# A fused attention, ELU and Mish kernel: the due times of its list scheduler moved by seeded noise

## The chip, the core and the metric

The kernel runs on one core of a Trainium2 chip. The metric is device time in microseconds (us) of one launch, the median of three runs. Five engines run side by side: PE (TensorE, matrix products and transposes), DVE (VectorE), ACT (ScalarE), POOL (GpSimd) and SP (SyncE, which here issues most DMAs). Each works off its own queue in the order in which the program was written, and waits where an operand or a buffer is not ready.

## The reference

```python
def _attn_ref(x, state):                       # x 4 x 8 x 512 x 64, state 4 x 8 x 32 x 64
    scale = 1.0 / np.sqrt(D)
    a = softmax(scale * np.matmul(x, state.transpose(0, 1, 3, 2)))
    xread = np.matmul(a, state)
    a2 = softmax(scale * np.matmul(state, x.transpose(0, 1, 3, 2)))
    sread = np.matmul(a2, x)
    return np.concatenate([xread, sread], axis=2)

def _moe_ref(x, w_in, w_out):                  # 2176 x 512, 512 x 2048, 2048 x 512
    h = x @ w_in
    g = np.where(h > 0.0, h, np.exp(np.minimum(h, 0.0)) - 1.0)
    return g @ w_out

def _moe2_ref(x, w_in, w_out):
    h = x @ w_in
    sp = np.where(h > 20.0, h, np.log1p(np.exp(np.minimum(h, 20.0))))
    return (h * np.tanh(sp)) @ w_out

x = attn(x, state)       # tokens and states attend to each other
x = x.transpose(0, 2, 1, 3).reshape(B * S, H * D)
out = moe2(moe(x))       # an ELU layer, then a Mish layer
```

(softmax stands for the reference's own lines: maximum off, exponential, division by the sum.)

## The kernel before, in words

The tokens of the four batches are four blocks (b = 0 to 3) of 512, and the 4 x 32 states make one small part more. For each block the kernel reads x in two halves of the heads (`load_x`, tile xb), transposes it on PE (xT, L641), forms the scores against the states (`score_tiles`, L653), copies them out (raw, L299, a helper that copies or casts on DVE or ACT), takes the softmax over the states on DVE and ACT (prob, L665 to L678) and transposes the result (L680; tile pT for b > 0, x for b = 0). It doesn't multiply the softmax by the states: it folds the states into the first weights (`fold`, L574), which gives m, and then h = softmax x m.

The ELU layer runs in steps of 128 of the 2048 hidden units for one block: `mm1` (h0, h1, ..., L782 to L793), `hidden` (ACT's exponential and a relu, DVE's e at L814, ACT's cast and DVE's low part, g), and `mm2` (L841 to L850), which adds g times w_out into four accumulators acc0 to acc3. The products are split: a value is a high part (fp32r) and a low part, so one product is three matmuls (such as L848, L849, L850). The first steps take whole fp32 values instead (L782, L841). The states' own reading (exT, sr, own, sT, L702 to L736) comes in between. Weights arrive as 64-bit floats and are turned into fp32 by two ACT instructions (wy L461, wv L463) and DVE's L466 and L478 or L503; the tiles w1_0 to w1_3 hold w_in of the ELU layer, each the source of one fold per block.

The Mish layer runs on two halves of the tokens in eight pairs of hidden tiles, with seven products per pair (prod, L1018) in the place of eight, and adds g times w_out into accA and accB (L1057 to L1059). Copies such as u2__0_1 (L1044, in the profile under u__0_1_832) take a product out of its bank. The last pieces of g are transposed on PE (turn16_0 to turn16_3, L1219) and multiplied last.

Every instruction is written through `Plan`, a list scheduler that runs on the host while the program is built. `add` registers an operation with its engine (or both DVE and ACT, EITHER: the scheduler takes the one that comes first), an assumed cost, and the tiles that it reads and writes. `dues` goes back from the end and gives each operation a due time: the earliest of what its successors allow, or a time given by hand from the table T of the steps. `run` then lays the program out in assumed time, always the operation that can start first, and of those with one start the one with the smaller due time:

```python
                    k = (t + late, due, seq, t)
```

PSUM has eight banks: two named "att" (xT, folds and others), two "h", and one for each of acc0 to acc3; an operation that has to place a tile waits until a bank of that tag is free. The two buffers wv serve the conversion of weights, and later hold u2 and c11 of the pairs. What stands on which place of an engine's queue is fixed when the program is built; on the chip it runs in that order whatever really is late.

## Time and profile before

| | before |
|---|---|
| median of 3 runs | 721.77 us (721.12 to 722.47) |
| profiled execution | 722.41 us, span 720.5 us |
| PE busy | 701.7 us, 97% |
| DVE busy | 556.7 us, 77% |
| ACT busy | 495.8 us, 69% |
| POOL busy | 3.0 us |
| DMA | 106.83 MB |

The profile is of one execution. Its span runs from the first to the last instruction, the time around it (1.9 us) belongs to the launch. A busy time counts instructions by their modelled lengths, and matmuls overlap, so a matmul of 0.39 us can follow the one ahead after 0.23 us. A timeline gives in brackets how long the engine stood idle ahead of an instruction and what released it.

### The profile page before, as it was taken

To read this page: it belongs to the slowest core of one execution; us is meant where nothing else is said; L and a number is where in the kernel's file an instruction comes from. 1 tells how busy PE (TensorE), PEld (TensorE's weight loads), DVE (VectorE), ACT (ScalarE), POOL (GpSimd) and SP (SyncE) were. 2 spreads that over 40 slices of the span, in tenths; PEclk is the share of its full clock that TensorE was granted. 3 is DMA by queue.
4 is the path that set the end of the run, shared out by engine and by line. 5 is a ranking of instruction groups with operands and counts; after the bars stand their busy time and mean duration, and the time that the engine had idled before them with its cause. 6 is when DMAs were issued, how large, how long until landed. Compare 5 with 4: busy or idle time off the path is not lost.

```text
span 720.5 us, 10191 instructions
## 1 busy us (share of the span) xinstructions
PE 701.7 (97%) x3698; PEld 546.3 (76%) x3698; DVE 556.7 (77%) x949; ACT 495.8 (69%) x861; POOL 3.0 (0%) x14
## 2 busy tenths in 40 slices
PE   5899999999989999999999999999999999999997
PEld 3345777777757778978887888878888888888886
DVE  6899988869879985447889998769738887767622
ACT  4797999768778776467868786669347666666522
POOL 0000000000000000000000000000000000000000
PEclk9799999999999999999999999999999999999999
DMA  9965556773685647106486454642035444401001
GB/s 224 276 180 138 128 174 227 234 234 99 209 258 167 200 146 246 51 20 229 164 279 225 150 147 127 221 163 58 1 117 147 136 127 125 142 27 58 15 1 58
DMA packets 65717, 106.83 MB, mean 148 GB/s; under 512 B 6660, under 2 KB 45572, under 8 KB 65668
## 3 DMA queue, kind: packets, MB, share of 16 engines
q1 hardware_dynamic: 63444, 105.53, 47.8%
q10 hardware_dynamic: 2224, 0.66, 0.4%
q8 instruction: 29, 0.48, 0.3%
q14 instruction: 20, 0.16, 0.1%
HBM read 78.38 MB, written 27.79 MB: 147 GB/s over the span
## 4 chain that ended last, share of the span: by engine, by line
PE 90%; DVE 7%; ACT 1%; issue 0%; DVEq 0%; ACTq 0%
PE prod L1018 20%; PE acc_acc L848 7%; PE acc_acc L850 7%; PE acc_acc L849 7%; PE accB L1057 4%; PE accB L1059 4%; PE accB L1058 4%; PE accA L1057 4%; PE accA L1059 4%; PE accA L1058 4%; PE h L791 3%; PE h L793 3%; PE h L792 3%; PE fold L574 2%; PE h L772 2%; PE acc_acc L841 2%
## 5 line engine op out<-in xcount | busy, mean ns | idle before, releaser
L1018 PE MATMUL prod<-x_t,pair 128*128 128x512 f32 x384 | 96.9, 390 | 0.5 <-ACT u__0_1_832_3916 L1044 0.5
L848 PE MATMUL acc_acc<-g,w_out 128*128 128x512 f32 x232 | 93.1, 401 | 0.0
L850 PE MATMUL acc_acc<-g,w_out 128*128 128x512 f32 x232 | 90.5, 390 | 0.0
L849 PE MATMUL acc_acc<-g,w_out 128*128 128x512 f32 x232 | 90.4, 390 | 0.0
L1018 PEld LDWEIGHTS prod<-x_t,pair 128*128 128x128 f32 x384 | 71.6, 188 | 15.5 <-ACT u__0_1_832_3916 L1044 1.0
L1018 PE MATMUL prod<-x_b,pair 128*128 128x512 f32 x288 | 72.4, 389 | 0.0
L976 ACT ACTIVATE e<-u,two 128x512 f32<-128x512 f32 x68 | 48.7, 722 | 21.7 <-DVE u L975 21.6
L1018 PEld LDWEIGHTS prod<-x_b,pair 128*128 128x128 f32 x288 | 54.1, 188 | 11.2
L814 DVE SCALAR_TENSOR_TENSOR e<-e,h 128x512 f32<-128x512 f32 x62 | 42.3, 683 | 25.5 <-ACT e L807 25.0
L806 ACT ACTIVATE e<-h 128x512 f32<-128x512 f32 x68 | 40.3, 595 | 26.2 <-PE h L793 17.3
L848 PEld LDWEIGHTS acc_acc<-g,w_out 128*128 128x128 f32 x232 | 43.7, 188 | 16.2 <-issue 5.4
L817 ACT CAST g<-e 128x512 fp32r<-128x512 f32 x62 | 38.4, 621 | 25.5 <-PE acc_acc L850 19.8
L978 DVE TENSOR_TENSOR u<-u,e 128x512 f32<-128x512 f32 x68 | 46.2, 687 | 12.0 <-ACT e L977 11.8
L818 DVE TENSOR_TENSOR g<-e,g 128x512 fp32r<-128x512 f32 x62 | 42.4, 685 | 14.6 <-ACT g L817 14.0
L850 PEld LDWEIGHTS acc_acc<-g,w_out 128*128 128x128 f32 x232 | 43.5, 188 | 9.3
L807 ACT ACTIVATE e<-e,one 128x512 f32<-128x512 f32 x68 | 49.2, 725 | 1.5
L1057 PE MATMUL accB<-w_out,g 128*128 128x512 f32 x128 | 50.0, 390 | 0.0
L849 PEld LDWEIGHTS acc_acc<-g,w_out 128*128 128x128 f32 x232 | 43.6, 188 | 8.4
L1059 PE MATMUL accB<-w_out,g 128*128 128x512 f32 x128 | 49.9, 390 | 0.0
L1058 PE MATMUL accA<-w_out,g 128*128 128x512 f32 x128 | 49.8, 389 | 0.0
L1059 PE MATMUL accA<-w_out,g 128*128 128x512 f32 x128 | 49.8, 389 | 0.0
L1058 PE MATMUL accB<-w_out,g 128*128 128x512 f32 x128 | 49.8, 389 | 0.0
(300 smaller groups left out, 1472.5 us busy)
## 6 DMA issues: line engine op xcount, KB each, us to landing
pair<-wi2d SPq DMA_DIRECT2D x64, 512.0 KB, 4.0
raw_out<-in_moe_w_out SPq DMA_DIRECT2D x32, 512.0 KB, 4.4
wi2d<-comb SPq DMA_DIRECT2D x64, 256.0 KB, 2.9
raw_in<-in_moe_w_in SPq DMA_DIRECT2D x32, 256.0 KB, 5.7
raw_in<-in_moe_w_in SPq DMA_DIRECT2D x16, 512.0 KB, 4.4
xb<-in_x SPq DMA_DIRECT2D x16, 256.0 KB, 4.9
x2d<-o SPq DMA_DIRECT2D x16, 256.0 KB, 3.9
out<-o SPq DMA_DIRECT2D x13, 256.0 KB, 2.5
```

The costliest lines, as they stand in the source:

```text
L807: add("ACT", act(n) + 0.12, lambda: nc.scalar.activation(E(), E(), AF.Relu, bias=one, scale=-1.0), r=[e, "one"], w=[e])
L814: add("DVE", dve(n), lambda: nc.vector.scalar_tensor_tensor(E(), E(), -1.0, Hh(), ALU.mult, ALU.max), r=[e, h], w=[e])
L818: add("DVE", dve(n), lambda: nc.vector.tensor_tensor(g[:, 1, :n], E(), g[:, 0, :n].bitcast(F32), ALU.subtract), r=[e, (g, 0)], w=[(g, 1)])
L848: nc.tensor.matmul(acc.t, lhsT=st[:, 0, :], rhs=mv[:, 0, :], start=fst, stop=False)
L849: nc.tensor.matmul(acc.t, lhsT=st[:, 0, :], rhs=mv[:, 1, :], start=False, stop=False)
L850: nc.tensor.matmul(acc.t, lhsT=st[:, 1, :], rhs=mv[:, 0, :], start=False, stop=lst)
L976: add("ACT", act(S) + 0.12, lambda: nc.scalar.activation(e.t, u.t, AF.Ln, bias=two), r=[u, "two"], w=[e])
L978: add("DVE", 0.69, lambda: nc.vector.tensor_tensor(u.t, u.t, e.t, ALU.mult), r=[u, e], w=[u])
L1018: nc.tensor.matmul(bank.t, lhsT=w[:, pos, a, c], rhs=x[b][:, k, :], start=first and k == i == 0, stop=k == 1 and i == 2, skip_group_check= ...
L1057: nc.tensor.matmul(acc.t, lhsT=g[:, 0, cols], rhs=w[:, 0, :], start=fst, stop=False)
L1058: nc.tensor.matmul(acc.t, lhsT=g[:, 0, cols], rhs=w[:, 1, :], start=False, stop=False)
L1059: nc.tensor.matmul(acc.t, lhsT=g[:, 1, cols], rhs=w[:, 0, :], start=False, stop=lst)
```

## The change

The scheduler's rule of choice stays, but each operation's due time gets a shift. `shifts` goes through a table MOVES of 41 pairs (seed, time). A pair draws, from its seed, a span of 6, 15 or 30 us, a size of 1, 3, 8 or 20 us and a share of 2, 10 or 30%; that share of the operations whose due time lies within the span after the given time is moved by Gaussian noise of that size. The table was found by laying the program out on the host. Of the 41 times 14 lie below 60, 6 from 110 to 209, 9 from 320 to 377, 7 from 406 to 478 and 5 above 628. Second, `go` (once part of `run`) counts PE's mode changes: folds, scores and the states' products use 32-row tiles (mode=1), and the first operation of the other mode costs 0.09 (in) or 0.2 (out) more in assumed time; their own assumed costs are lowered for it. Third, `combine` names its operands' writers as predecessors. The rest makes the layout repeatable and quicker to compute. A filler of PE's gaps, which was switched off, is gone.

```diff
+INTO, OUT_OF = 0.09, 0.2
+MOVES = ((75118, 15.0), (37424, 20.5), (643, 25.2), (75746, 1.9), (30105, 6.6), (37635, 33.7), (41153, 30.7), (49481, 4.2), (3259, 37.4), (47714, 34.4), (99535, 58.8), (1855, 44.2), (56018, 54.5), (88942, 41.2), (59791, 110.1), (52383, 208.2), (23200, 178.9), (15004, 167.9), (91882, 181.8), (18113, 161.2), (20944, 353.0), (89527, 345.3), (66176, 375.8), (92493, 376.6), (76941, 320.4), (42889, 369.3), (68313, 348.7), (27382, 356.5), (3732, 353.0), (87073, 460.2), (93436, 406.0), (26739, 418.9), (55693, 443.5), (55858, 447.2), (21623, 477.8), (29573, 460.3), (85558, 628.6), (12285, 659.9), (62500, 655.4), (81304, 657.9), (63908, 660.6))
...
-    def add(self, engs, cost, fn, r=(), w=(), due=None, lag=0.0, after=(), place=()):
+    def add(self, engs, cost, fn, r=(), w=(), due=None, lag=0.0, after=(), place=(), mode=0):
...
-    def run(self, take, dma):
-
-        self.dues(dma)
+    def go(self, dma, shift, take=None, until=1e9):
...
-                ready.setdefault(e, []).append((op.due, op.seq, t, op))
+                ready.setdefault(e, []).append((due, op.seq, t, op, wait))
...
+            due = op.due + shift.get(op.seq, 0.0)
...
-            if e == "PE" and t < COLD_UNTIL:
-                c *= COLD
+            op.at = t
+            if e == "PE":
+                if t < COLD_UNTIL:
+                    c *= COLD
+                if op.mode != mode:
+                    c += INTO if op.mode else OUT_OF
+                    mode = op.mode
...
+    def shifts(self, moves):
+
+
+        shift = {}
+        for seed, a in moves:
+            rng = random.Random(seed)
+            span, sd, share = rng.choice((6, 15, 30)), rng.choice((1, 3, 8, 20)), rng.choice((0.02, 0.1, 0.3))
+            for op in self.ops:
+                if a <= op.due < a + span and rng.random() < share:
+                    shift[op.seq] = shift.get(op.seq, 0.0) + rng.gauss(0, sd)
+        return shift
+
+    def run(self, take, dma):
+        self.dues(dma)
+        self.go(dma, self.shifts(MOVES), take)
+        assert self.end < math.inf, "stuck"
...
-    add("DVE", 3.2, make_ident, w=["ident"], due=-50.0)
+    add("DVE", 2.4, make_ident, w=["ident"], due=-50.0)
...
-            add("DVE", 0.43, lambda: nc.vector.tensor_tensor(o(), a(), b(), op), r=r, w=w, place=[sa, sb])
+            add("DVE", 0.43, lambda: nc.vector.tensor_tensor(o(), a(), b(), op), r=r, w=w, place=[sa, sb],
+                after=[plan.writer[a1], plan.writer[a2]])
...
-            A("PE", 0.1 + mm(4 * step * P), lambda j=j: f(j), w=[(pt, j) for pt in pts], place=[*ms, *pts],
+            A("PE", 0.05 + mm(4 * step * P), lambda j=j: f(j), mode=1, w=[(pt, j) for pt in pts], place=[*ms, *pts],
...
-        A("PE", 0.65, score_tiles, r=[(xT, 0), (xT, 1), ("sd", b)], w=ps, lag=lag, place=held)
+        A("PE", 0.45, score_tiles, mode=1, r=[(xT, 0), (xT, 1), ("sd", b)], w=ps, lag=lag, place=held)
...
-        A("PE", 1.0, read, r=[(xb, 0), (xb, 1), exT], w=[pt])
+        A("PE", 0.5, read, mode=1, r=[(xb, 0), (xb, 1), exT], w=[pt])
```

What moves is read from the order of the instructions on each engine. A row is the line, the operation, output and inputs, and the shape; the last number of a name is a serial number, which shifts between the two programs. Lines of the changed kernel are up to 40 higher.

The first place is the start of PE's queue: the first transposes of block 0 (xT12, xT13, xT21, xT22), those of the states (st2 to st4) and the first scores. Before:

```order
L641 MATMUL xT12_127<-ident_69,xb0_5_102 128x128 x4
L641 MATMUL xT13_133<-ident_69,xb0_5_102 128x128 x4
L411 MATMUL st2_139<-ident_69,st_raw1_100 128x128 x2
L411 MATMUL st3_146<-ident_69,st_raw1_100 128x128 x2
L641 MATMUL xT21_150<-ident_69,xb0_16_107 128x128 x4
L653 MATMUL scores14_157<-xT7_128,sd0_77 32x256
...
L641 MATMUL xT22_172<-ident_69,xb0_16_107 128x128 x4
L411 MATMUL st4_184<-ident_69,st_raw1_100 128x128 x4
L653 MATMUL scores23_194<-xT17_151,sd0_77 32x256
```

With the change:

```order
L679 MATMUL xT12_124<-ident_69,xb0_5_102 128x128 x4
L448 MATMUL st2_133<-ident_69,st_raw1_100 128x128 x2
L448 MATMUL st3_137<-ident_69,st_raw1_100 128x128 x2
L679 MATMUL xT13_141<-ident_69,xb0_5_102 128x128 x4
L448 MATMUL st4_147<-ident_69,st_raw1_100 128x128 x4
L679 MATMUL xT21_155<-ident_69,xb0_16_107 128x128 x4
L691 MATMUL scores14_163<-xT7_125,sd0_77 32x256
...
L691 MATMUL scores24_200<-xT17_156,sd0_77 32x256
L679 MATMUL xT160_227<-ident_69,xb153_153 128x128 x4
L612 MATMUL fold142_248<-w1_0_28_240,sd0_77 32x128
```

Both pairs of state transposes now stand ahead of xT13, st4 ahead of xT21, and xT160, the transposes of the first half of block 1's tokens, between the scores and the first fold.

The second place is DVE's queue up to pT175, the transposed softmax of the second half of block 1's tokens. Before, its last twelve rows:

```order
L689 TENSOR_TENSOR x1_1_154_636<-pT164_640,x1_1_154_636 128x512
L818 TENSOR_TENSOR g227_659<-e226_630,g227_659 128x512
L665 STREAM_TRANSPOSE prob167_647<-raw168_648 128x512
L671 TENSOR_REDUCE mx169_649<-prob167_647 128x16
L672 TENSOR_TENSOR prob167_647<-prob167_647,mx169_649 128x512
L466 SCALAR_TENSOR_TENSOR wv100_674<-wy99_673,wv100_674 128x512
L478 SCALAR_TENSOR_TENSOR w1_2_86_661<-wy92_607,wv93_608 128x4x128
L675 TENSOR_REDUCE sm170_650<-prob167_647 128x16
L676 TENSOR_SCALAR sm170_650<-sm170_650 128x16
L677 RECIPROCAL sm170_650<-sm170_650 128x16
L678 TENSOR_TENSOR prob167_647<-prob167_647,sm170_650 128x512
L680 STREAM_TRANSPOSE pT175_732<-prob167_647 128x2x2x128
```

With the change:

```order
L703 STREAM_TRANSPOSE prob167_622<-raw168_623 128x512
L852 SCALAR_TENSOR_TENSOR e226_615<-e226_615,h7_221_600 128x512
L709 TENSOR_REDUCE mx169_624<-prob167_622 128x16
L710 TENSOR_TENSOR prob167_622<-prob167_622,mx169_624 128x512
L503 SCALAR_TENSOR_TENSOR wv85_612<-wy84_611,wv85_612 128x512
L856 TENSOR_TENSOR g219_663<-e218_602,g219_663 128x512
L713 TENSOR_REDUCE sm170_625<-prob167_622 128x16
L856 TENSOR_TENSOR g227_680<-e226_615,g227_680 128x512
L714 TENSOR_SCALAR sm170_625<-sm170_625 128x16
L715 RECIPROCAL sm170_625<-sm170_625 128x16
L716 TENSOR_TENSOR prob167_622<-prob167_622,sm170_625 128x512
L718 STREAM_TRANSPOSE pT175_698<-prob167_622 128x2x2x128
```

The weight words wv100 and the piece of w1_2 no longer stand between the softmax's rows; g219 and e226, which stood higher, do.

The third place is PE around the fold of w1_2 for block 2 (fold474, fold475), the transposes of block 3's tokens (xT503, xT504, xT514, xT515) and their scores. Before:

```order
L574 MATMUL fold474_2192<-w1_2_86_661,sd2_79 32x512
L574 MATMUL fold475_2193<-w1_2_86_661,sd2_79 32x512
L641 MATMUL xT503_2220<-ident_69,xb496_2055 128x128 x4
L641 MATMUL xT504_2229<-ident_69,xb496_2055 128x128 x4
L848 MATMUL acc1_2_acc2_534_2237<-g494_2036,w_out1_0_193_390 128x512
...
L653 MATMUL scores506_2252<-xT498_2221,sd3_80 32x256
L641 MATMUL xT514_2268<-ident_69,xb508_2069 128x128 x4
L641 MATMUL xT515_2275<-ident_69,xb508_2069 128x128 x4
L848 MATMUL acc1_2_acc3_535_2283<-g494_2036,w_out1_0_193_390 128x512
```

With the change:

```order
L612 MATMUL fold475_2111<-w1_2_86_733,sd2_79 32x512
L829 MATMUL h34_525_2129<-x1_2_293_1792,m2_0_0_384_1770 128x512
...
L831 MATMUL h40_589_2367<-x1_2_293_1792,m2_8_1_473_2113 128x512
L679 MATMUL xT515_2374<-ident_69,xb508_2125 128x128 x4
L829 MATMUL h40_589_2367<-x1_2_293_1792,m2_8_0_472_2112 128x512
...
L888 MATMUL acc1_2_acc0_532_2145<-g581_2334,w_out1_6_75_618 128x512
L679 MATMUL xT514_2395<-ident_69,xb508_2125 128x128 x4
L886 MATMUL acc1_2_acc1_533_2155<-g581_2334,w_out1_6_75_618 128x512
...
L691 MATMUL scores517_2414<-xT509_2375,sd3_80 32x256
L829 MATMUL h41_606_2429<-x1_2_293_1792,m2_8_0_472_2112 128x512
L830 MATMUL h41_606_2429<-x1_2_293_1792,m2_8_0_472_2112 128x512
L831 MATMUL h41_606_2429<-x1_2_293_1792,m2_8_1_473_2113 128x512
L679 MATMUL xT504_2436<-ident_69,xb496_2107 128x128 x4
```

The fold is now followed by step 34's h, the transposes come 110 rows later and one by one, and three matmuls of h41 stand between the scores and the next transposes.

## Rows read from the trace of the kernel before

**Rows 1.** The page: the chain that ended last, shares of the span by engine.

```profile
PE 90%; DVE 7%; ACT 1%; issue 0%; DVEq 0%; ACTq 0%
```

**Rows 2.** The table by windows: busy us (instructions) per engine, granted clock, DMA share, GB/s.

```profile
11.00:15.30 4.30, 0.82 (x12) 0.17 (x9) 4.09 (x9) 3.26 (x8) 0.00 (x0) 1.00 1.14 223
15.30:25.70 10.40, 6.77 (x38) 2.28 (x38) 8.68 (x18) 5.86 (x14) 0.00 (x0) 0.51 1.09 277
...
50.00:80.00 30.00, 28.58 (x174) 16.36 (x174) 29.14 (x54) 25.18 (x48) 1.16 (x2) 1.00 0.57 145
...
200.00:215.00 15.00, 13.03 (x99) 8.19 (x98) 10.65 (x18) 10.30 (x22) 0.21 (x1) 1.00 0.84 265
...
sum 720.50, PE 701.70 PEld 546.34 DVE 556.70 ACT 495.78 POOL 3.03; mean PE 53.98 PEld 42.03 DVE 42.82 ACT 38.14 POOL 0.23
```

**Rows 3.** Timeline of PE, 69 to 77 us: start, length, instruction, idle time before it.

```profile
69.26 0.39 PE L849 MATMUL acc_acc<-g,w_out 128*128 128x512 f32 x1
...
70.84 0.39 PE L850 MATMUL acc_acc<-g,w_out 128*128 128x512 f32 x1
71.16 1.09 PE L574 MATMUL fold<-w,sd 64*32 64x512 f32 x16
73.00 0.50 PE L791 MATMUL h<-x,m 128*128 128x512 f32 x1 [0.75 <-ACT x L299]
73.73 0.50 PE L792 MATMUL h<-x,m 128*128 128x512 f32 x1 [0.23 <-DVE x L689]
...
76.72 0.50 PE L791 MATMUL h<-x,m 128*128 128x512 f32 x1 [0.44 <-DVE e L814]
```

**Rows 4.** Timeline of PE, 201 to 209 us.

```profile
201.85 1.09 PE L574 MATMUL fold<-w,sd 64*32 64x512 f32 x16
204.40 1.25 PE L641 MATMUL xT<-ident,xb 128*128 128x128 f32 x8 [1.46 <-DVE m L588]
...
208.36 1.09 PE L641 MATMUL xT<-ident,xb 128*128 128x128 f32 x8 [0.52 <-ACT raw L299]
```

**Rows 5.** Timeline of PE at three later waits.

```profile
242.96 0.33 PE L736 MATMUL sT<-ident,own 128*128 128x128 f32 x1 [0.27 <-DVE own L730]
...
382.03 1.65 PE L1018 MATMUL prod<-x_t,pair 128*128 128x512 f32 x6 [0.55 <-ACT u__0_1_832_3916 L1044]
...
661.74 0.65 PE L1219 MATMUL turn<-ident,g 128*128 128x128 f32 x4 [0.56 <-DVE g L987]
```

**Rows 6.** Timeline of PE in the first 30 us.

```profile
7.30 1.08 PE L411 MATMUL st<-ident,st_raw 128*128 128x128 f32 x4
...
8.93 0.66 PE L653 MATMUL scores<-xT,sd 64*32 64x256 f32 x16
...
15.31 0.49 PE L574 MATMUL fold<-w,sd 64*32 64x128 f32 x2 [3.32 <-DVE w L478]
...
20.36 2.08 PE L782 MATMUL h<-x,m 128*128 128x512 f32 x2 [1.17 <-DVE x L680]
...
26.75 1.13 PE L782 MATMUL h<-x,m 128*128 128x512 f32 x2
```

**Rows 7.** Timeline of DVE in the first 24 us.

```profile
22.10 0.70 DVE L680 STREAM_TRANSPOSE x<-prob 128x512 f32<-128x512 f32 x1
```

**Rows 8.** Timeline of DVE, 71 to 76 us.

```profile
71.19 0.71 DVE L680 STREAM_TRANSPOSE pT<-prob 128x512 f32<-128x512 f32 x1
...
75.98 0.68 DVE L814 SCALAR_TENSOR_TENSOR e<-e,h 128x512 f32<-128x512 f32 x1
```

**Rows 9.** Groups of DVE instructions: busy us, mean ns, idle time before.

```profile
L478 DVE SCALAR_TENSOR_TENSOR w<-wy,wv 128x512 uint32<-128x512 uint32 x16 | 10.8, 678 | 0.2
...
L299 DVE COPY xT<-xT 128x512 f32<-128x512 f32 x3 | 2.1, 689 | 4.0 <-PE xT L641 4.0
...
L299 DVE COPY sd<-st 128x256 f32<-128x256 f32 x2 | 0.8, 419 | 0.9 <-PE st L411 0.9
```

**Rows 10.** Timeline of ACT around 381 us.

```profile
381.39 0.59 ACT L1044 COPY u__0_1_832_3916<-prod 128x512 f32<-128x512 f32 x1 [0.62 <-DVE w_out L503]
```

More of the change, by code (lines that the diff above doesn't have):

```diff
@@ L2 @@
 import math
+import random
 from contextlib import ExitStack
@@ L71 @@
 class Op:
-    __slots__ = ("engs", "cost", "fn", "preds", "succs", "bufs", "due", "n", "end", "lag", "seq")
+    __slots__ = ("engs", "cost", "fn", "preds", "succs", "bufs", "due", "n", "end", "lag", "seq", "need", "key", "mode", "at")
 class Plan:
@@ L141, in run @@
         link = 0.0
+        LAT = self.LAT
+        for op in self.ops:
+            op.n, op.end = op.need, None
+            for b in op.bufs:
+                b.t, b.left, b.end = None, b.uses, 0.0
         def open_op(op):
@@ L153, in run @@
         todo = len(self.ops)
+        mode, pe, idle = 0, [], 0.0
         while todo:
@@ L157, in run @@
                 at = free.get(e, 0.0)
-                cand, first = None, None
-                for due, seq, t, op in lst:
-                    if op.end is not None:
+                slow = e in ("DVE", "ACT")
+                if e in dma and link - BACKLOG > at:
+                    at = link - BACKLOG
+                if best and at > best[0][0]:
+                    continue
+                for due, seq, t, op, wait in lst:
+                    if t < at:
+                        t = at
+                    if best and t > best[0][0]:
@@ L178, in run @@
                     late = 0.0
-                    if e in ("DVE", "ACT"):
-                        late = LAZY if due - t > FAR else 0.0
+                    if slow:
+                        if due - t > FAR:
+                            late = LAZY
                         if e == "DVE" and len(op.engs) > 1 and at > 80.0:
@@ L232, in run @@
             for x in op.engs:
-                ready[x] = [q for q in ready[x] if q[3] is not op]
+                lst = ready[x]
+                for i, q in enumerate(lst):
+                    if q[3] is op:
+                        del lst[i]
+                        break
             for s in op.succs:
```

91 lines of the change are left out of this document (43 added, 48 removed).

## The prediction

> **What bounds the kernel now.** I read the page first, for the chain that ended last: TensorE (PE) holds 90% of it, VectorE (DVE) 7% [rows 1]. Then the table by windows, whose last line says that PE is busy 701.7 of 720.5 us [rows 2]. So PE is the bound over the run as a whole, and another order of the same work can only win back time in which PE issues nothing, at most some 19 us. The windows also say where that time lies. After the first 26 us PE falls visibly short in two stretches, 28.58 of 30 us in 50 to 80 and 13.03 of 15 us in 200 to 215. In 50 to 80 DVE is busy 29.14 of 30 us: there DVE is the bound, and PE waits for it. Last the timeline of PE at each such place, which names the wait.
>
> A 128x512 matmul issues every 0.226 us: the eight from 69.26 to 70.84 are 1.58 us for seven steps. The first one after a wait lasts 0.50 instead of 0.39 us [rows 3], so I charge each wait its idle time and 0.11 us. The profiled execution took 722.41 us, 1.9 more than its span of 720.5; the median of the three runs is 721.77, 0.64 lower. The sum is formed against 722.41, and 0.64 taken off at the end.
>
> **What the waits are worth.** After the start they are these.
> - A, 71 to 77 us: behind a fold PE waits 0.75 us for ScalarE's (ACT's) cast of the second half of block 1's tokens, 0.23 us for DVE's low part of it, and further on 0.44 us for DVE's e of step 8 [rows 3]. With 3 x 0.11 that is 1.75 us.
> - B, 201 to 208 us: a fold, right behind it two transposes xT, then scores, and two more xT. Both pairs need the two "att" banks that the work ahead of them still holds: 1.46 us until DVE has read the fold (m), and 0.52 us until ACT has copied the scores (raw) [rows 4]. With 2 x 0.11 that is 2.2 us.
> - Later: 0.27 us at 242.96 (sT needs DVE's own), 0.55 us at 382.03 (product t3 needs the bank that ACT's copy u2__0_1 empties), 0.56 us at 661.74 (the fourth turn needs DVE's g) [rows 5]. With 0.11 each: 0.38, 0.66 and 0.67 us.
>
> Together 5.7 us; this is the most that another order can return after the start.
>
> **What the change does at each place.** The work, the tiles and the number of matmuls (2647 rows of PE's order) are as before. Positions move, and some copies change between DVE and ACT.
>
> *Start: 0 us (-1 to +1).* PE waits here: 3.32 us before the fold at 15.31, then for x [rows 6]. The granted clock is 1.00 in 11.0 to 15.3, where PE is busy 0.82 of 4.3 us, and 0.51 in 15.3 to 25.7, the lower of its two levels, 1.2 GHz [rows 2]. The change puts st2 and st3 ahead of xT13. They start at 7.30 and last 1.08 us [rows 6], and they wait for the states, which arrive only then; so xT13 starts after 8.2 us, and the first scores, now at 8.93, come about 0.9 us later, by xT13's own transposes and its copy. That is the loss. On the other side DVE, which is filled from 11 us on (4.09 of 4.3, then 8.68 of 10.4 us [rows 2]), loses one weight word of 0.6 us from ahead of the second transpose x at 22.10 [rows 7] and gains a copy of about the same. So x stays near 22.1. Both ends are cushioned: from 26 us to A PE runs without a wait, and there it waits for DVE, so up to 1.7 us of delay on PE alone is taken up at A, and an earlier start of PE alone brings nothing.
>
> *A: -0.8 us (0 to -1.75).* DVE is full, so what counts is the work queued on it ahead of pT175, at 71.19 [rows 8]: 119 instructions before, 117 after. Five whole-tile words leave (wv93, wv100, two pieces of w1_2, the low part of w_out 5), 0.68 us each; of copies and casts six leave and nine come, two of the three more at 0.42 and one xT at 0.69 [rows 9]. That is -3.4 + 1.5, about -1.8 us at the pace of a full queue. It would remove the first two waits, 1.2 us. But the e of step 8, at 75.98 now [rows 8], moves up only from place 123 to 122 of the queue, so the third wait stays and may grow by 0.2; and a group of three matmuls (0.68 us) that PE ran after A now comes ahead of it, where it may wait itself. I take 0.8, less than half of the bound.
>
> *B: -2.0 us (-1.2 to -2.2).* The fold of w1_2 goes ahead by some 40 matmuls and is followed by h34, which reads an m finished long before; the transposes of block 3 come 110 rows later, with no fold near, the first between two halves of h40. The pair behind scores now has three matmuls, 0.68 us, in between, more than the 0.52 waited. So neither wait has its cause left; 0.2 stays for the two pairs' own use of the banks.
>
> *242 us: -0.2 (0 to -0.38).* sT now comes three matmuls after the last product of the states (sr) instead of six. The chain from sr to own is as long, so part of the wait may stay.
>
> *382 us: -0.6 (0 to -0.66).* ACT's copy u2__0_1 was idle 0.62 us for DVE's conversion w_out [rows 10], since both use the two buffers wv. After the change that conversion no longer stands right ahead of it. Against it: the last steps of the ELU layer now alternate with the first products of the Mish layer, which must find their banks empty.
>
> *661 us: -0.6 (0 to -0.67).* Before, the four turns stand in a row, and the fourth waits. After, turn16_0 comes six matmuls earlier, and turn16_3 stands behind nine matmuls of the last part, 2.0 us more for DVE's g.
>
> *New waits: +0.5 (0 to +2).* The tokens of block 2 are the tightest: between their scores and the second half of h32 PE has 42 matmuls, one fold and a few transposes, some 12.7 us, where it had 15.2, and DVE has to do a chain of ten instructions in it, beside the others in its queue. Two folds stand 12 matmuls (2.7 us) apart, and casts and differences of the first take some 2. The acc of step 3 may wait 0.6 us for its weights. I expect one of these to bite.
>
> *Mode changes: 0.* From the last L850 to the fold at 71.16 is 0.32 us instead of 0.226 [rows 3]: entering a stretch of 32-row matmuls costs 0.09 us. PE has 33 such stretches before and 35 after, and the two more lie ahead of 25 us, where PE waits anyway. The Trainium skill, "TensorEngine Tiling (Array Packing)", Key Properties, says that a change of the tiling mode drains the engine; the 0.09 us agrees with it. By that rule alone, two stretches more, the change would cost time: at some 0.2 us for both ends of one, +0.4 us.
>
> Sum: 0 - 0.8 - 2.0 - 0.2 - 0.6 - 0.6 + 0.5 = -3.7 us. 722.41 - 3.7 = 718.7 for a profiled execution, 718.1 us as a median.
>
> **The rivals.**
> - *All waits go.* A loses its third wait too, nothing new appears, and DVE gains up to 1 us at the start, which A passes on: 721.77 - 5.7 - 1 = 715.1. Against it: DVE's queue is as full as before, and e of step 8 hardly moves. One more way leads here: two h matmuls take 2.08 us at 20.36, at the low clock, and 1.13 at 26.75 [rows 6]. If the four transposes xT160, now put into the idle stretch between scores and fold, kept the clock up, over 0.95 us would come back on PE, though A would take most of it. The Trainium skill, "TensorE: Matmul & The Clock Gate", Part 4, says that transposes don't count as busy for the clock, which speaks against that; no trace here shows it yet.
> - *Waits only move.* The 5.7 us are waits for DVE and ACT, whose work is unchanged. Where PE arrives earlier it waits later: at h32 (up to 2), the first Mish products (up to 1), the acc of step 3 (0.6). Then the 3.7 are paid back: 721 to 722. For it: DVE's 29.14 of 30 us. Against it: in 200 to 215 DVE is busy 10.65 of 15 us [rows 2], so B was a matter of order, not of load.
> - *Slower: the start.* One mechanism: the first scores wait for the states behind st2 and st3. If the first x comes over 1.7 us later, A's cushion is used up, and each further us shows, since DVE's whole queue moves back with it; the low clock also lasts longer, 0.95 us per pair of h matmuls. Three us late with two more pairs at the low clock is 3 + 1.9 - 1.7 = 3.2, less B's 2.0: +1.2 and more, 723 to 724. It decides from some 2.5 us of delay at the scores; I count 0.9.
>
> **How the numbers follow.** A measurement of this kernel can tell about 0.2%, 1.44 us, from no change. Likeliest is the sum, with some terms off: 0.62, with a range of its own of 716.8 to 720.3. All waits go: 0.12. Waits only move: 0.16, most of it within 1.44 us. Slower: 0.10. Faster by over 0.2% takes the first two and a little of the third, 0.77; same 0.13; slower 0.10. The range reaches from the rival with all waits gone, 715.0, to near the middle of the second, 721.5.
>
> **What would show it.** Right: no PE wait behind a fold for DVE's m around 200 us, and PE near 15 of 15 us there; the waits for the fourth turn and for u2__0_1 gone; at A the cast of x no longer waited for, but e of step 8 still. Wrong: a PE wait for the tokens of block 2, or for acc near 60 us; the first fold or h over a microsecond later than 15.3 and 20.4; a low clock that lasts beyond 26 us.

## The result, and the profile after

The changed kernel takes 715.19 us (median of 4 runs, 714.15 to 716.58), the kernel before beside it 721.44 us (721.02 to 722.47): a ratio of 0.9912, 95% interval 0.9888 to 0.9937. That is 6.25 us less, where 3.7 were forecast; 715.19 lies just inside the range (715.0 to 721.5) and close to the rival that all waits go (715.1). The four runs fall into two groups, 714.15 and 714.23, 716.15 and 716.58; the experiments below show where that comes from. The profiled execution is one of the slower two, 716.58 us with a span of 714.6.

The page of the changed kernel: busy time by engine, and the chain that ended last, which answers to [rows 1].

```profile
PE 700.1 (98%) x3698; PEld 547.1 (77%) x3698; DVE 557.3 (78%) x951; ACT 493.3 (69%) x859; POOL 3.5 (0%) x14
...
PE 97%; DVE 1%; DMA 1%; ACT 0%; issue 0%
```

PE holds 97% of the chain and DVE 1%, where they held 90% and 7%. The table by windows answers to [rows 2]: busy time (instructions) of PE, PE's weight loads, DVE, ACT and POOL, then the granted clock, the DMA share and GB/s.

```profile
11.00:15.30 4.30, 3.70 (x40) 1.54 (x39) 3.12 (x6) 2.53 (x6) 0.00 (x0) 1.00 1.13 240
15.30:25.70 10.40, 4.67 (x36) 1.82 (x37) 10.40 (x22) 6.84 (x15) 0.00 (x0) 0.70 1.10 265
...
50.00:80.00 30.00, 30.00 (x173) 17.25 (x172) 29.55 (x55) 24.00 (x46) 1.16 (x2) 1.00 0.45 123
...
200.00:215.00 15.00, 15.00 (x68) 12.43 (x67) 10.28 (x17) 10.44 (x17) 0.00 (x0) 1.00 0.81 244
```

Both stretches in which PE fell short are full, 30.00 of 30 and 15.00 of 15 us. DVE is as busy in 50 to 80 us as before, 29.55 us for 29.14. PE's waits of the whole run, grouped, tell the same: every line belongs to the first 22 us.

```profile
PE fold L612 <- DVE w L515: 4.7, 1, 4.7
PE warm L410 <- DVE ident L396: 3.1, 1, 3.1
PE h L820 <- DVE sm L715: 1.4, 1, 1.4
PE st L448 <- DMA st_raw<-in_state: 0.9, 1, 0.9
PE scores L691 <- ACT xT L339: 0.3, 1, 0.3
```

The timeline of PE at A, which answers to [rows 3]:

```profile
66.32 1.09 PE L612 MATMUL fold<-w,sd 64*32 64x512 f32 x16
67.33 0.50 PE L886 MATMUL acc_acc<-g,w_out 128*128 128x512 f32 x1
...
72.24 0.39 PE L829 MATMUL h<-x,m 128*128 128x512 f32 x1
72.47 0.39 PE L830 MATMUL h<-x,m 128*128 128x512 f32 x1
...
74.97 0.60 PE L751 MATMUL exT<-ident,raw 128*128 128x128 f32 x4
75.37 0.50 PE L829 MATMUL h<-x,m 128*128 128x512 f32 x1
```

A fold stands at 66.32 and is over some five microseconds ahead of the h at 72.24; before, a fold stood right ahead of the h that waited. The h matmuls from 72.24 on follow each other at 0.23 us. The timeline of DVE there, which answers to [rows 8]:

```profile
69.24 0.71 DVE L718 STREAM_TRANSPOSE pT<-prob 128x512 f32<-128x512 f32 x1
...
74.64 0.68 DVE L852 SCALAR_TENSOR_TENSOR e<-e,h 128x512 f32<-128x512 f32 x1
```

pT came 1.95 us earlier (69.24 against 71.19) and the e of step 8 1.34 us earlier (74.64 against 75.98). The remaining places on PE, which answer to [rows 4] and [rows 5]:

```profile
188.27 1.09 PE L612 MATMUL fold<-w,sd 64*32 64x512 f32 x16
189.29 0.50 PE L829 MATMUL h<-x,m 128*128 128x512 f32 x1
...
192.23 1.09 PE L612 MATMUL fold<-w,sd 64*32 64x512 f32 x16
...
218.56 0.60 PE L679 MATMUL xT<-ident,xb 128*128 128x128 f32 x4
...
246.95 0.27 PE L774 MATMUL sT<-ident,own 128*128 128x128 f32 x1
...
657.54 0.60 PE L1257 MATMUL turn<-ident,g 128*128 128x128 f32 x4
657.89 0.48 PE L1095 MATMUL acc<-w_out,g 128*128 128x512 f32 x1
```

The folds are each followed by h matmuls, the transposes stand one by one, and sT and the turns have no wait in front.

**A ledger.** A timeline's brackets count only idle time past the modelled end of an instruction. So I also went through PE's queue and added up the step at which each kind of matmul issues when nothing holds it (0.227 us for a 128x512 of a split product, 0.43 for one of whole fp32, 0.109 for a transpose). The time on the clock minus that sum is the time lost so far. Here it is at several times, for the kernel before, and for each other run as its difference to before; the e-numbers are the experiments below. In the last two rows the added transposes (38 and 42 of 0.109 us) have been put back, so that all rows mean the same. The first column is the least certain, since the folds and the clock of the start weigh most there.

```
at us                  30     70     80    200    260    360    390    470    500    670
before, lost        19.81  25.26  27.85  31.70  36.39  37.45  38.23  38.11  38.71  40.09
changed kernel        0.1    0.8   -1.4   -1.2   -4.2   -4.2   -5.0   -5.0   -5.6   -6.3
e1 (the same)        -1.2   -1.8   -4.0   -3.9   -6.8   -6.8   -7.6   -7.6   -8.2   -8.9
e2                   -0.7   -0.9   -3.1   -2.9   -5.9   -5.9   -6.7   -6.7   -7.3   -8.0
e8                   -0.6   -0.2   -2.4   -2.1   -5.0   -5.0   -5.8   -5.8   -6.5   -7.1
e6 (120 to 285)       0.2    0.5    0.5    0.7   -2.1   -2.1   -2.1   -2.1   -2.1   -2.1
e7 (from 285)        -0.5   -1.0   -1.0   -1.0   -1.0   -1.0   -1.8   -1.8   -2.4   -3.1
e12 (up to 285)      -1.0   -1.3   -3.5   -3.3   -6.3   -6.3   -6.3   -6.3   -6.3   -6.3
e10                  -0.3    0.1   -2.1   -1.9   -4.9   -4.9   -5.7   -5.7   -6.3   -7.0
e11                  -1.1   -1.7   -1.5   -1.4   -1.4   -1.4   -1.4   -1.4   -1.4   -1.4
```

The changed kernel gains 2.2 us at A (between 70 and 80), 3.0 between 200 and 260, 0.8 at 382, 0.6 between 470 and 500, and 0.7 at 661. In between, the difference moves by 0.2 us at most. The order of before isn't one row of zeros either: e6 and e7 have it up to 120 and 285 us, and stand 0.5 behind and 1.0 ahead of the trace of before at 70 us. The end (from the last matmul to the end of the span) went from 4.1 to 4.4 us.

### The profile page after: what moved, and what is told of

Same layout as the page of the kernel before. It is cut to its first block, busy times and chain, and to the rows that moved or that the text cites. A ratio compares the mean times of both kernels' runs of the same rounds, so it can differ in the third digit from the quotient of the medians.

```text
span 714.6 us, 10194 instructions
## 1 busy us (share of the span) xinstructions
PE 700.1 (98%) x3698; PEld 547.1 (77%) x3698; DVE 557.3 (78%) x951; ACT 493.3 (69%) x859; POOL 3.5 (0%) x14
## 4 chain that ended last, share of the span: by engine, by line
PE 97%; DVE 1%; DMA 1%; ACT 0%; issue 0%
PE prod L1056 21%; PE acc_acc L886 8%; PE acc_acc L888 7%; PE acc_acc L887 7%; PE accA L1095 4%; PE accB L1096 4%; PE accA L1096 4%; PE accB L1097 4%; PE accB L1095 4%; PE accA L1097 4%; PE h L829 4%; PE h L831 4%; PE h L830 4%; PE acc_acc L879 3%; PE h L820 2%; PE fold L612 2%
## 5 line engine op out<-in xcount | busy, mean ns | idle before, releaser
L1016 DVE TENSOR_TENSOR u<-u,e 128x512 f32<-128x512 f32 x68 | 46.5, 688 | 16.0 <-ACT e L1015 15.3
```

What stands on the lines that cost most here:

```text
L1016: add("DVE", 0.69, lambda: nc.vector.tensor_tensor(u.t, u.t, e.t, ALU.mult), r=[u, e], w=[u])
```

## The experiments

Throughout, theory 1 is that each place is worth the wait that goes there and the parts add up; theory 2 is that waits only move, because DVE's and ACT's work is the same. For the start, theory 1 is that its length passes to the end of the run, theory 2 is the prediction's cushion at A.

**e1, the same kernel again.** No edit.

> The changed kernel once more, for its size and its spread: its four runs lay at 716.2 to 716.6 twice and at 714.2 twice. Theory 1 (the two levels come from the start, where the granted clock rises once early, once late; in the profile at hand it rises at 12.65 us, before it rose at 8.61): a profile at 714.2 shows the first scores and the first h up to 2 us earlier and everything after 30 us as in the profile at hand. Theory 2 (a wait in the middle that appears in some executions): the start is the same in both, and one wait of some 2 us after 30 us is there in the slower one only.

714.15 us (714.09 to 716.16), 0.9896 (0.9879 to 0.9912), again in two groups, three executions near 714.1 and one at 716.16. The median lies below the range of the prediction. The profiled execution is now one of the faster, with a span of 712.1. Two timelines of PE's start, first the changed kernel's, then e1's:

```profile
7.29 1.09 PE L448 MATMUL st<-ident,st_raw 128*128 128x128 f32 x4 [0.93 <-DMA st_raw<-in_state]
...
10.87 1.11 PE L691 MATMUL scores<-xT,sd 64*32 64x256 f32 x16
...
19.66 0.68 PE L612 MATMUL fold<-w,sd 64*32 64x128 f32 x16 [4.69 <-DVE w L515]
21.70 2.04 PE L820 MATMUL h<-x,m 128*128 128x512 f32 x2 [1.37 <-DVE sm L715]
```

```profile
7.28 0.63 PE L448 MATMUL st<-ident,st_raw 128*128 128x128 f32 x4 [0.98 <-DMA st_raw<-in_state]
...
9.17 0.66 PE L691 MATMUL scores<-xT,sd 64*32 64x256 f32 x16
...
17.52 0.68 PE L612 MATMUL fold<-w,sd 64*32 64x128 f32 x16 [2.41 <-DVE w L515]
19.56 2.05 PE L820 MATMUL h<-x,m 128*128 128x512 f32 x2 [1.36 <-DVE sm L715]
```

The instructions are the same. In the first the four transposes st take 1.09 us, in e1 0.63, and the first scores 1.11 and 0.66. I read this as the two levels of the clock: the first still ran at the lower one past 10 us, e1 had left it by 7.28. (The granted clock reads 1.00 in both there; only the durations tell them apart.) The scores come 1.7 us earlier in e1, and the first h 2.1. From the first scores to the first h it is 10.8 and 10.4 us, and before it was 11.4 (8.93 to 20.36 [rows 6]): DVE is busy in most of it, 9.54 of the 10.83 us in the first and 9.61 of 10.39 in e1, and its instructions from 12.07 us on (9.93 in e1) stand 2.1 us earlier throughout. So an early rise at 7 us reaches the first h by way of DVE, and the ledger shows 2.6 us between the two executions at 70 us and the same 2.6 at 670.

**e2, xT13 ahead of the state transposes again.**

```diff
+        xt13, sts = self.first
+        for st in sts:
+            st.preds.append(xt13)
+            st.need += 1
+            xt13.succs.append(st)
...
```

> The changed kernel with the first transposes of PE in the order of before (xT13 ahead of the states' st2 and st3, st4 behind xT22); nothing else on PE, DVE or ACT moves beyond these. Theory 1 (the states' transposes ahead of xT13 delay the first scores from 8.93 to 10.87 us and the first h from 20.36 to 21.70, and nothing takes that up, since the changed order has no wait left at 72 us): 1 to 2 us faster than the changed kernel, about 713 to 714. Theory 2 (the delay is taken up by DVE's full queue up to 80 us, as the prediction held for the kernel before): no difference, 714 to 716.5.

714.78 us (714.41 to 715.85), 0.9900 (0.9886 to 0.9914): no difference. Its first scores at 8.65 and first h at 19.36 are earlier than e1's, but its low clock ended at 25.2 us where e1's ended at 23.2.

**e3, only the moves from 110 to 209.**

```diff
-MOVES = ((75118, 15.0), (37424, 20.5), (643, 25.2), (75746, 1.9), (30105, 6.6), (37635, 33.7), (41153, 30.7), (49481, 4.2), (3259, 37.4), (47714, 34.4), (99535, 58.8), (1855, 44.2), (56018, 54.5), (88942, 41.2), (59791, 110.1), (52383, 208.2), (23200, 178.9), (15004, 167.9), (91882, 181.8), (18113, 161.2), (20944, 353.0), (89527, 345.3), (66176, 375.8), (92493, 376.6), (76941, 320.4), (42889, 369.3), (68313, 348.7), (27382, 356.5), (3732, 353.0), (87073, 460.2), (93436, 406.0), (26739, 418.9), (55693, 443.5), (55858, 447.2), (21623, 477.8), (29573, 460.3), (85558, 628.6), (12285, 659.9), (62500, 655.4), (81304, 657.9), (63908, 660.6))
+MOVES = ((59791, 110.1), (52383, 208.2), (23200, 178.9), (15004, 167.9), (91882, 181.8), (18113, 161.2))
```

> The changed planner with only the six moves at times 110 to 209 kept. B is then as in the changed kernel (the fold of w1_2 ahead, the transposes of block 3 far behind it), and the Mish layer's end as before. By the ledger of the two traces (waits at 201 to 243 us are worth 2.9 us): 718.5 if the start and 71 to 77 us stay as before; the waits at 382, 484 and 661 us stay in the profile, about 0.8, 0.6 and 0.7 us. If the wins hang together (a later stretch moved by all that comes ahead), under 717 or over 720.

724.54 us (722.59 to 727.49), 1.0037 (1.0025 to 1.0049): slower, on the side on which the wins were to hang together (over 720). PE's waits at 200 to 215 us are gone. Two others are there that neither kernel has, and the wait for the e of step 8 is longer than before (1.1 for 0.44 us), in the grouped waits of PE:

```profile
PE prod L1056 <- ACT u__0_2_856_4064 L1082: 2.3, 1, 2.3
PE prod L1056 <- ACT u__0_4_900_4356 L1082: 1.1, 1, 1.1
PE h L829 <- DVE e L852: 1.1, 1, 1.1
```

By the same sums, which the table leaves out, e3 gains 2.7 us between 200 and 260 us and keeps them to 360, close to the 2.9 expected; it loses 0.8 ahead of 70 us, 0.3 at A and 4.1 between 390 and 470. So the waits at B were not paid back; the new ones come from places where a shorter table leaves another order. The table isn't a sum of edits: a subset of it lays the whole program out anew. No run has the changed scheduler with an empty table, so how much of the order is owed to the noise and how much to the new assumed costs stays open. To test parts, the finished orders had to be cut and joined instead (e5 on).

**e4, only B's edit.** Kernel before, with block 3's transposes held back behind steps 38 and 39.

```diff
+STEPS = ((38, 1), (39, 1))
...
+        for hf, op in self.later:
+            p = self.steps[STEPS[hf]]
+            op.preds.add(p)
+            p.succs.append(op)
+            op.n += 1
...
```

> The kernel before with one thing moved: the transposes of block 3's tokens have to come after step 38 (first half) and step 39 (second half), so that they stand between halves of h40 and h41 and not behind a fold. Theory 1 (the waits at 204.4 and 208.4 us are a matter of that order alone and nothing takes their place): 2.2 us by the sum of the prediction, up to 2.9 by the ledger, so 718.5 to 719.2. Theory 2 (the waits move to where DVE or ACT are needed next): 720.5 to 721.5, with new PE waits between 205 and 250 us.

724.28 us (723.49 to 724.8), 1.0027 (1.0015 to 1.0039): slower than either theory had it. The transposes wait no longer, and others do, in the timeline of PE:

```profile
201.49 1.09 PE L581 MATMUL fold<-w,sd 64*32 64x512 f32 x16
204.03 1.68 PE L581 MATMUL fold<-w,sd 64*32 64x512 f32 x16 [1.45 <-DVE m L595]
...
208.96 0.50 PE L857 MATMUL acc_acc<-g,w_out 128*128 128x512 f32 x1 [1.66 <-DVE half L895]
```

The fold of w1_3 now stands right behind that of w1_2 and waits until DVE has read that one's product (m), and a matmul of acc waits until DVE has taken the accumulator's last sum out (half). The mechanism is theory 2's: the wait moved on to the next instructions that needed a bank or DVE, and by the same sums 2.1 us more than before are lost between 200 and 212 us. In the changed kernel the two folds are 4 us apart (188.27 and 192.23).

**e5, the first 120 us.** From here on the order in which one of the two kernels issued its 2938 operations is written into the program as a table, and `run` only goes through it; a kernel of two parts takes the operations of one order up to a time and then what is left in the order of the other.

```diff
...
+        for word in ORDER.split():
+            op = self.ops[int(word.rstrip("AD"))]
+            for b in op.bufs:
+                if b.t is None:
+                    b.t = take(b)
+            op.fn({"A": "ACT", "D": "DVE"}[word[-1]]) if len(op.engs) > 1 else op.fn()
...
```

> The order of the changed kernel up to 120 us, and from there on word for word the order of the kernel before (operations written in a fixed order, without the planner). Theory 1 (the parts add up): the wins at the start and at 71 to 77 us alone, by the ledger 1.4 us where the granted clock rises late and 3.9 where it rises early, so 718.0 to 720.8 in two levels; the waits at 204, 208, 243, 382, 484 and 661 us are all there, as long as before. Theory 2 (what is won early is waited for later): the same time as before, with the waits at 204 and 208 us longer.

725.44 us (724.7 to 728.47), 1.0054 (1.0039 to 1.0068). The ledger shows -3.6 at 80 and 100 us, but PE then waits 5.07 us at 125.78 for a copy of exT that stands on the wrong side of the cut. At this cut, laid at 118 us, the two orders have not issued the same operations. As a test of the sum it is inconclusive; A's own gain, -2.1 between 70 and 80, is there.

**e6, the middle part alone**: before to 120 us, the changed order to 285, before behind it (the same edit with another table; at 285 us there is a place at which both orders have issued exactly the same operations, while the cut at 120 us is not clean, but made no wait here).

> The order of before up to 120 us, of the changed kernel from there to 285 us, of before again to the end (at 285 us both orders have written the same operations). Theory 1: the waits at 204, 208 and 243 us go and nothing takes their place, since here the folds and weights move along with the transposes, other than in the experiment that moved the transposes alone: 2.9 us, 719.3. Theory 2 (the gain there hangs on the earlier part): under 1.5 us, with a PE wait of over 1 us between 150 and 285.

719.15 us (718.73 to 720.19), 0.9961 (0.9949 to 0.9973). The timeline of PE shows the waits at A, 382 and 661 us as before, and none between 80 and 379. By the ledger -2.8 us between 200 and 260, near the 2.9 expected:

```profile
73.55 0.50 PE L800 MATMUL h<-x,m 128*128 128x512 f32 x1 [0.75 <-ACT x L308]
...
77.26 0.50 PE L800 MATMUL h<-x,m 128*128 128x512 f32 x1 [0.43 <-DVE e L823]
...
379.91 1.42 PE L1027 MATMUL prod<-x_t,pair 128*128 128x512 f32 x5 [0.54 <-ACT u__0_1_832_3916 L1053]
...
659.60 0.66 PE L1228 MATMUL turn<-ident,g 128*128 128x128 f32 x4 [0.56 <-DVE g L996]
```

**e7, the last part alone**: before to 285 us, the changed order behind it.

> The order of before up to 285 us, where both have written the same operations, and the changed one from there. Theory 1: the waits at 382, 484 and 661 us go, by the ledger 0.8 + 0.6 + 0.7 = 2.1 us, so 720.1, and the others stay. Theory 2 (in the changed kernel these waits went since PE came there earlier or later than before): a smaller gain, with waits at the first Mish products.

721.08 us (719.77 to 721.37), 0.9981 (0.9972 to 0.9989). The waits at 382 and 661 us are gone and so is the loss at 484; 2.1 us by the ledger from 285 us on, as expected, of which the end, 4.6 us after the last matmul for 4.1, takes 0.5 back.

**e8, 14 warm transposes in place of 10**, so that PE doesn't idle ahead of st.

```diff
-        add("PE", 0.24 * WARM, lambda: turns(pt, WARM), r=["ident"], w=[pt], due=-40.0)
+        add("PE", 0.24 * WARM, lambda: turns(pt, WARM + 4), r=["ident"], w=[pt], due=-40.0)
```

> The changed kernel with 14 instead of 10 warming transposes ahead of the first xT (four more of 0.21 us, 0.85 us, which is what PE waits for the states at 6.4 us); every other instruction stays in its place. Theory 1 (PE's idle time of 0.93 us ahead of the states' transposes is what lets the granted clock rise only at 12 us in some executions): the upper level of the changed kernel's times, 716.2 to 716.6, is gone, and the median is 714.1 to 714.8. Theory 2 (the two levels have nothing to do with that idle time): both levels still occur, the median between 714.2 and 716.4.

714.43 us (714.26 to 716.32), 0.9892 (0.9878 to 0.9907), in the same two groups. Its profiled execution is the slow one, 716.32 us, and PE has no idle time ahead of st in it: that idle time isn't what makes the groups.

**e9, the first 149 us** (as e5, cut at another place).

> The order of the changed kernel up to about 149 us (so with stretch A's waits gone), the order of before behind it, with the cut laid where no instruction is left over on the wrong side. Theory 1, the parts add up: by the trace of the changed kernel the first 150 us are worth -1.4 us when the first low-clock stretch ends late and up to -3.9 us when it ends early, so 718.0 to 720.8 us, and the waits at 204, 208, 242, 382, 484 and 661 us stand as in the kernel before. Theory 2, waits only move: what is gained at 75 us is waited for again at B or later, longer waits there than before and a time of 721 to 722 us.

727.77 us (725.58 to 729.7), 1.0077 (1.006 to 1.0094). Again the cut, at which the two orders have not issued the same operations, makes a wait of its own, in the timeline of PE:

```profile
161.18 1.97 PE L650 MATMUL xT<-ident,xb 128*128 128x128 f32 x8 [5.21 <-DVE m L597]
```

The later waits can't be read behind it. A's gain is there again, -2.1, and keeps to 140 us.

**e10, the changed order with transposes put into PE's idle time at the start**, into a bank not yet in use (F18 is 18 of them; part of the table's first two lines).

```diff
+0D 1 4 13 2 5 14 32 3 33 61 15 51 6 16D 8 7A 17 9D 10 18D 246 34 11D 12A 19 71 35D 36 20D 21A 23A 22D 24D 37A 81 25D 62A 38 F18 63A 41D 40A 39D 42A 64D
+26A 56 43D 52A 27D 53A 248 F12 44D 54D 91 45A 28D 55D 249A 29D 72A 46D 231 F8 233A 30D 101 232A 73A 47D 31D 48D 65D 286 49D 66 82A 234 74D 83A 50D 235A
```

> The changed kernel with added transposes of no use in PE's idle time at the start (18 behind the first scores, 12 behind block 0's last xT, 8 behind the first fold), written into a PSUM bank not yet in use. Theory 1, the low clock between 16 and 26 us comes from PE's idling before it: the clock stays at 1.00 there, the h matmuls take 0.43 us each from the first on, and the time is about 712.5 to 713.5 us at one level. Theory 2, transposes do not keep the clock up, or DVE sets the pace there: the low stretch stands as before and so do the two levels, 714.1 to 716.4 us.

715.67 us (713.34 to 717.05), 0.9903 (0.9887 to 0.9919): no gain over the changed kernel in the median, though its two fastest executions, 713.34 and 713.43, lie below the lowest of the changed kernel (714.09). Theory 1 fell in part: the low stretch became shorter, 0.84 as the mean clock in 15.3 to 25.7 us for 0.70, but the first scores were at 11.13 and the first h at 21.62, late as in the changed kernel's profiled execution, so this trace can't tell what the filling does behind an early start.

**e11, the order of before with such transposes** (22, 12 and 8).

> The kernel before with the same kind of added transposes (22, 12 and 8). The prediction's reading: PE's delay at the start is taken up at stretch A, where it waits for DVE anyway, so that an earlier or faster start of PE alone brings nothing: 721 to 722.5 us, with longer waits near 75 us. Rival: DVE's own work near 75 us hangs on the early matmuls, and the start passes to the end in part: 1 to 1.5 us less, 720 to 720.5 us.

720.94 us (720.53 to 722.55), 0.9986 (0.9978 to 0.9995). The table by windows, then the timeline of PE at A:

```profile
15.30:25.70 10.40, 7.67 (x75) 3.99 (x74) 9.16 (x20) 6.61 (x16) 0.00 (x0) 1.00 1.11 260
...
50.00:80.00 30.00, 28.56 (x175) 16.84 (x174) 29.52 (x55) 25.23 (x47) 1.16 (x2) 1.00 0.58 144
```

```profile
69.64 1.09 PE L590 MATMUL fold<-w,sd 64*32 64x512 f32 x16
71.48 0.50 PE L807 MATMUL h<-x,m 128*128 128x512 f32 x1 [0.75 <-ACT x L314]
72.23 0.50 PE L808 MATMUL h<-x,m 128*128 128x512 f32 x1 [0.25 <-DVE x L705]
...
75.22 0.50 PE L807 MATMUL h<-x,m 128*128 128x512 f32 x1 [0.43 <-DVE e L830]
```

The low clock that stood in 15.3 to 25.7 us (0.51 in [rows 2]) is gone. The first h comes at 20.23, 0.13 us earlier only, but the first two h last 1.12 us together, not 2.08 [rows 6], and the fold ahead of A starts 1.52 us earlier (69.64 for 71.16). At A the three waits are as long as in [rows 3], 0.75, 0.25 and 0.43 us, and all of A is 1.5 us earlier, pT at 69.69 for 71.19 with it. So A is no cushion: DVE's work ahead of it hangs on PE's, and moves with it. e6 and e7 say the same without added work: the order is that of before there, and the 0.5 behind and the 1.0 ahead at 70 us are unchanged at 80. The rival's saving of 1 to 1.5 us was right (1.2 by the medians), its 720 to 720.5 us a little too low.

**e12, the first 285 us**, cut where nothing is out of place.

> The order of the changed kernel up to about 285 us, that of before behind it: at this place both orders have issued nearly the same set of operations, so the cut should leave nothing waiting. Theory 1, the parts add up: the middle part alone gave -2.3 us and the last part alone -0.6 to -1.3, and the whole -6 to -7; the rest, stretch A with the start, is worth about -2 to -3, so this kernel gives -4.5 to -6: 715.8 to 717.5 us, at two levels some 2 us apart like the changed kernel's, PE waiting for nothing between 30 and 285 us, and the waits at 382, 484 and 661 us as in the kernel before. Theory 2, what is won at A is waited for later: 719 us, no better than the middle part alone.

717.41 us (716.06 to 718.1), 0.9939 (0.9925 to 0.9952). PE's waits after the start, in its timeline, are those of before in the last part, and none else:

```profile
375.72 1.45 PE L1027 MATMUL prod<-x_t,pair 128*128 128x512 f32 x5 [0.54 <-ACT u__0_1_832_3916 L1053]
...
655.49 0.66 PE L1228 MATMUL turn<-ident,g 128*128 128x128 f32 x4 [0.56 <-DVE g L996]
```

-6.3 by the ledger at 260 us, and it stays there to the end. Theory 1: the parts add up. Behind its start e12 gains 5.0 us up to 260 us, as e1 does, and e7 gains 2.1 from 285 us on, as e1 does. The medians tell it less sharply, since the start spreads by some 2 us: 4.7 us for e12 and 1.3 for e7, against 6.3 and 8.2 for the whole.

## Why the prediction was right and wrong

The direction, the places and the mechanism were right: the time lay in PE's waits at A, B and the three later places, which were a matter of order, and it came back. The time was inside the range, but 2.9 us below the forecast and 0.2 above the range's lower end, and the same kernel run again (e1) took 714.15 us, below it. That the first measurement fell inside was luck: two of its four executions were of the slower group, one of the four in e1. By the steps:

- **A, forecast -0.8 (0 to -1.75), measured -2.2.** This is the largest miss. e5, e9, e12 and every full version give -2.1 to -2.2, more than the bound. Two things were wrong. The e of step 8 was to stay late because it stood one place earlier in DVE's queue only; it came 1.34 us earlier, since the whole queue ahead of it had become shorter, as pT shows (1.95 us; -1.8 had been worked out). I had the number and halved it. (No run changes DVE's queue alone, so this is read from the two traces; that the gain at A comes with the order of the first 285 us is what e12 tests.) And the bound, idle time and 0.11 us per wait, left out what the modelled length hides: before, the first h at A started at 73.00 and the second at 73.73 [rows 3]. That is a step of 0.73 for one of 0.227, so 0.50 lost, with 0.23 shown as idle and 0.34 charged.
- **B and 242 us, forecast -2.2, measured -3.0** between 200 and 260 (-2.8 in e6, -3.0 in e12). From start to next start, the fold took 2.55 us before and takes 1.02 in the changed kernel, the eight transposes behind it 1.19 for 0.79, the scores 1.18 for 0.59, and the last h ahead of sT with sT 0.75 for 0.26. So the first wait was worth 1.9 us, where 1.57 were charged (the transposes behind it were slow too), the second 0.6 as charged, and sT 0.5 for 0.38.
- **382 and 661 us, forecast -0.6 each, measured -0.8 and -0.7.** Right.
- **484 us, not in the sum, measured -0.6.** The brackets showed nothing there. The timeline of PE of the kernel before:

```profile
483.94 0.39 PE L1059 MATMUL accA<-w_out,g 128*128 128x512 f32 x1
484.35 0.50 PE L1057 MATMUL accB<-w_out,g 128*128 128x512 f32 x1
484.69 0.39 PE L1058 MATMUL accB<-w_out,g 128*128 128x512 f32 x1
485.08 0.51 PE L1059 MATMUL accB<-w_out,g 128*128 128x512 f32 x1
485.42 0.40 PE L1057 MATMUL accB<-w_out,g 128*128 128x512 f32 x1
```

The steps are 0.41, 0.34, 0.39 and 0.34 us where 0.227 is the rule, 0.57 us lost without a bracket. ACT's cast of the g that they read ran from 483.68 us on, behind three copies o; in the changed kernel's order of ACT the first cast stands ahead of the copies, and these matmuls of accB follow at 0.23 us. Those casts in the timeline of ACT, first before:

```profile
483.68 1.30 ACT L986 CAST g<-late 128x512 fp32r<-128x512 f32 x2
```

and in the changed kernel, with the first copy o at 477.33:

```profile
476.65 0.63 ACT L1024 CAST g<-late 128x512 fp32r<-128x512 f32 x1
```

So the time in which PE shows as idle, some 19 us, which the prediction took for the most that another order can return, is no such bound.
- **New waits, forecast +0.5, measured 0.** The tokens of block 2, the two folds and the acc of step 3 don't wait: PE has no wait after 22 us. This was the one term put in without a row, for what might happen. e3 and e4 show that such waits are real for other orders; the changed kernel's order has none.
- **Start, forecast 0 (-1 to +1), cushioned at A; measured +0.8 or -1.8 at 70 us against the trace of before, not cushioned.** Most of that difference isn't the change's, since the order of before starts early or late too. In e7 its four st took 0.63 us, its first h came at 19.75 and PE was 1.0 us ahead of the trace of before at 70 us; in e6 they took 1.09 us, the first h came at 20.75 and PE was 0.5 behind. Early against early (e1 and e12 against e7), the changed order is 0.3 to 0.8 us ahead at 70 us; late against late (its profiled execution against before and e6), 0.3 to 0.8 behind. So the number held. The scores came 0.24 us later than in the trace of before with the early clock (e1, 9.17) and 1.94 later with the late one (10.87); 0.9 was forecast. From there to the first h it takes 0.6 to 1.0 us less. The cushion was the step that failed: across e1, e2, e8, e10, e12 and the changed kernel's own profile A gains 2.1 to 2.2 us whether PE comes to it 1.8 us earlier or 0.8 later, and e6, e7 and e11 show the same with A's waits in place. The signs that the prediction gave against itself, a first fold after 16.3 (19.66), a first h after 21.4 (21.70) and a low clock past 26 us (26.3), all appeared in the profiled execution, and weren't decisive: the start decides 2 us, the waits 7.
- **Mode changes, forecast 0.** No loss of over 0.2 us appears outside of these places. The +0.4 us that the prediction works out for two more stretches wasn't seen, though the start's spread would cover it.

By these numbers the sum is -2.2 - 3.0 - 0.8 - 0.6 - 0.7 = -7.3, and +0.8 to -1.8 for the start and +0.3 to +0.5 at the end: -6.2 to -8.6 in the span, where -5.9 and -8.4 were measured. That is bookkeeping, since the terms are read from the same traces; the tests of it are e6, e7 and e12. The medians lie at -6.3 and -8.2 us in the two sets of runs of this kernel, and the executions of the kernel before spread as well (721.02 to 723.06 over all of them).

Of the rivals, "all waits go" is what happened. That its 715.1 us was met so closely is luck: it put 5.7 us on the places, which gave 7.3, and 1 us on the start, which gave none in that execution. "Waits only move" is what e4 did, with another order. The third, a late start, showed up at a quarter of its size (0.8 of the 3.2 us).

**The two groups** fit two numbers of the start in the five profiled executions of the changed order (e2, e8 and e10 with their edits at the start), the first h and the end of the low clock, both different from execution to execution (the latter from windows of 1 us). Half the time between them counts as lost on PE, as the h matmuls take about twice as long there (2.08 us for two, for 1.13 [rows 6]). The first h and that half add up to 21.4 us for e1 (19.56, low to 23.2), 22.3 for e2 (19.36, 25.2), 23.3 for e10 (21.62, 25.0), 23.4 for e8 (20.44, 26.3) and 24.0 for the profiled changed kernel (21.70, 26.3); the spans are 712.1, 713.1, 714.0, 714.3 and 714.6. What decides whether the clock rises before or after st is open: the same kernel did both.

## What to carry to other kernels

Where one engine is the bound, make the ledger first: its work at free-running steps against the clock, place by place. It finds waits that brackets hide (0.57 us at 484) and gives them their true size (A was 1.5 times its idle time), and it shows at which place a change pays and whether it keeps. An engine that is full isn't by that a cushion: if its queue hangs on the other engine, an early start passes through it whole. And a good order is a whole: parts cut out at a place where both orders have done the same work add up, to 0.1 us by the ledger behind the start, while one edit alone (e4) moved the waits, and a part of the table (e3) won its own place and lost more elsewhere.

## What the runs showed that was not expected

- The transposes kept the clock up in e11. Before, the granted clock was 0.72 in 15 to 16 us and 0.50 behind it, after PE had idled 3.32 us; in e11 the same stretch, with transposes only put into the idle time, stayed at 1.00, and the h matmuls ran at the higher level from the first on. The Trainium skill, "TensorE: Matmul & The Clock Gate", Part 4, says that a transpose doesn't count as busy in the same way; this trace doesn't agree, if these transposes, which the profile lists as MATMUL, run in the mode that the page means. In e10 the clock fell all the same, later (0.80 in 21 to 22 us, 0.50 from 22 to 25, 0.99 behind it); why is open.
- A wait of 5 us in the middle of the run costs more than itself: in e5 PE waits up to 125.78 us for exT, the granted clock is 0.57 as the mean of 122 to 130 us, and the first h matmuls behind the wait follow each other at 0.43 us. By the sums of the ledger 6.1 us more than before are lost between 120 and 130 us, for 5.07 of idle time.
- By the length of the transposes st (0.63 or 1.09 us for four) the clock's first rise comes before 7.3 us in some executions and later in others, past 10 us in the changed kernel's profile; the granted clock's column reads 1.00 in both.
